# Copying the FFN's PSUM banks to SBUF on ScalarE before VectorE adds to them

## The chip, the cores and the metric

The kernel runs on one core of a Trainium2 chip. The time is the device time of one execution in microseconds (us), taken as the median over repeated executions. The profile is a single execution recorded by the hardware profiler; it has its own time, and a span from its first to its last instruction.

Five engines work in parallel, each on its own queue in order: TensorE (PE in the profile; its weight loads are PEld), VectorE (DVE), ScalarE (ACT), GpSimd (POOL) and SyncE (SP, which here only issues transfers). TensorE writes its products into PSUM, eight banks of 128 x 512 float32 values; VectorE and ScalarE read them from there. Everything else lies in SBUF. An engine that needs what another one made waits on a semaphore at the head of its queue, and all that stands behind it in that queue waits too.

## The reference, cut to what matters

Input `x` has 2048 tokens of 512 channels. Two branches are computed from it and mixed by a gate per token:

```
g = sigmoid((x * gate_w).sum(-1, keepdims=True))
q, k, v = split(x @ wqkv)                      # 32 heads of 16 channels
idx = pos[:, None] - arange(8)[None, :] * 2    # each token sees 8 tokens, 2 apart
logits = where(idx >= 0, einsum(q, k[idx]) * 16**-0.5, -1e9)
a = einsum(softmax(logits), v[idx]) @ wo
b = (gelu(x @ w_gate) * (x @ w_up)) @ w_down   # 512 -> 1792 -> 512
return g * a + (1 - g) * b
```

All data are float32.

## The kernel before, in words

**Tokens and passes.** The tokens are taken in two passes (`par` 0 and 1: the even and the odd ones), 1024 tokens each. A pass projects keys and queries (`project`, `qkv_mm`, L247), then values (`values`, L298), and then runs the FFN (`ffn`). The attention itself is done by VectorE (`scores`, `softmax`, `mix`, L390 to L453) and is written as one long generator, `attention`. `pull` takes pieces of it between the FFN's pieces, so that VectorE's attention work lies beside TensorE's FFN work over nearly the whole run.

**Float32 on TensorE.** Each operand is split into a high part and a remainder, and a product takes three matmuls (high x high, low x high, high x low).

**The FFN's first half.** `ffn` loops over 14 tiles `f` of 128 hidden columns; each calls `gate_up`. There the tokens (two halves of 512), the channels (two halves of 256) and the columns (gate and up) form a 2 x 2 by 2 x 2 block product, which is done with seven block products instead of eight. One block product, `product` (L600 to L606, its matmuls on L605), is six matmuls 128 x 128 by 128 x 512 into one bank. The operands of the tokens are `A` tiles (plain blocks a11, a12, a22) and `S` tiles (sums s1 to s4); the weights lie in `g0` and `g1`. The order in one tile `f` is:

1. `X_` = a11 b11; ScalarE copies it into a second bank `W_` (L680).
2. `Z_` = s1 t1; ScalarE copies it to SBUF as `p5` (`copy`, L610).
3. `fourth()`: the seventh product of the tile before, a22 t4, is added into that tile's `X_`; ScalarE applies gelu to it (L711), and `hidden` follows.
4. `X_` += s2 t2; ScalarE copies it to SBUF as `u2`.
5. `W_` += a12 b21; ScalarE applies gelu (L695), giving `c11`.
6. `Z_` += s4 b22; then `c12 = add(Z_, u2)`.
7. `X_` += s3 t3; then `c22 = add(X_, p5)`; `X_` stays in use until step 3 of the next tile.

`add` (L613 to L616) is called twice for each tile, 28 times in a pass and 56 times in all. It takes a tile of the pool `c` (four buffers) for its result. The bank that it reads can be written again only when the read is over: `Z_` goes back into the rotation of four banks called `p`, and the seventh product goes on adding into `X_`.

`hidden` (L618 to L623) multiplies the gelu by the up part on VectorE (L619), takes the high part on ScalarE (`hh`, L621) and the remainder on VectorE (`hl`, L622).

**The FFN's second half.** `down` (L634 to L660) multiplies `hh` and `hl` by the down weights `d` (matmuls on L645). For half the tokens the sums stay in the banks `acc0` to `acc3`; for the other half they go through `p` banks that ScalarE fills from SBUF (L639) and empties again into `rt` (L658). The pieces of `down` stand between the steps above.

**Other ScalarE work in a tile.** It makes the weights' parts for the tiles ahead: `operands` (L554, L562, L565) and `down_w` (L591, L595, L598). Keys and queries of the second half of the heads are copied out of their banks on L268 and sent to HBM on SP's queue (L271), from which `load_kq` (L379, L382) and `load_slots` bring them back for the attention. VectorE makes the other part of `g0` on L558 and sums of weights on L534.

**What sets the order.** The program is written in the order above, but the framework's scheduler places each engine's instructions by its own timeline when the kernel is built, so an edit can move instructions on any queue. `paced` ties an instruction to the last matmul written before it, for the scheduler alone.

Of the kernel before, what the change touches and what calls it, by code (L numbers as in the profile page):

```python
# [12 lines left out]
AF = mybir.ActivationFunctionType  # L13
OP = mybir.AluOpType
# [30 lines left out]
def tile_gated_mix(ctx: ExitStack, tc: tile.TileContext, xt, wqkv, wff, wo, out):  # L45
    nc = tc.nc
# [10 lines left out]
    def tl(tag, dt=F32):  # L57
        return pool.tile([P, COLS.get(tag, 512)], dt, name=tag, bufs=BUFS[tag])
# [5 lines left out]
    def bank(tag):  # L64
        return psum.tile([P, 512], F32, name=tag, bufs=BUFS.get(tag, 1))
# [545 lines left out]
        return s  # L611

    def add(ps, s):  # L613
        c = tl("c")[:, :512]
        nc.vector.tensor_tensor(c, ps, s, op=OP.add)  # L615
        return c  # L616

    def hidden(key, ge, up):  # L618
# [43 lines left out]
    def gate_up(par, f, pieces, do):  # L662
# [33 lines left out]
        idle(5, 0.7)  # L696
        product(Z_, "s4", w["b22"], False)
        c12 = add(Z_, u2)
        idle(6, 0.5)
        piece(2)  # L700
        product(X_, "s3", w["t3"], False)
        c22 = add(X_, p5)
        hidden((f, 0), c11, c12)
        idle(7, 0.7)
# [180 lines left out]
    def finish(oT):  # L885
        def add(u, jj):
            half, t = divmod(jj, BT)
            by_unit(ACC[jj], oT[u, half], u, t, False, u == NU - 1)

        for u in range(NU - 1):  # L890
            need_o(1, u + 1)
            for half in range(2):
                oT[u + 1, half] = channels(1, u + 1, half)
            if u + 2 < NU:
                for jj in range(NP):
                    add(u, jj)
                pull(4.0)

        for jj in range(BT):
            add(NU - 2, jj)  # L900
        for jj in range(NP):
            if jj >= BT:
                add(NU - 2, jj)
            add(NU - 1, jj)
            pa = ACC.pop(jj)
            r = tl(("s", "rt")[jj % 2])
            if jj % 2 and jj < NP - 1:
                nc.vector.tensor_copy(r, pa)
            else:
                nc.scalar.activation(r, pa, AF.Copy)  # L910

            cols = ((nc.scalar, 0, 256), (nc.sync, 256, 512)) if jj == NP - 1 else ((nc.sync, 0, 512),)
            for queue, a, b in cols:
                queue.dma_start(out_v[2 * jj + 1, :, a:b], r[:, a:b])
# [21 lines left out]
    ps = [bank(next(names)) for _ in range(NP)]  # L936
# [108 lines left out]
```

## Time and profile before

| | |
|---|---|
| median of 3 runs | 614.03 us (612.59 to 614.57) |
| profiled execution | 614.4 us, its span 612.6 us |
| TensorE busy, 2791 matmuls | 599.9 us, 98% of the span |
| VectorE busy, 624 instructions | 531.1 us, 87% |
| ScalarE busy, 643 instructions | 375.6 us, 61% |
| chain that ended last | PE 79%, DVE 7%, DMA 7%, ACT 3%, issue 3% |
| mean granted TensorE clock | 0.994 |

A row of a group reads: line, engine, operation, output<-inputs, sizes, count | busy us, mean ns of one | idle us of the engine just before them, and what ended it. A row of the timeline reads: start us, us, engine, line, operation, output<-inputs, count, and in brackets the idle time before it with its releaser. The ends of matmuls are modelled: consecutive ones overlap in the rows, so their pace is read from their starts. Instructions of VectorE and ScalarE overlap their neighbours in the rows by about 0.1 us as well.

### The profile page before, as it was taken

To read this page: it belongs to the slowest core of one execution; us is meant where nothing else is said; L and a number is where in the kernel's file an instruction comes from. 1 tells how busy PE (TensorE), PEld (TensorE's weight loads), DVE (VectorE), ACT (ScalarE), POOL (GpSimd) and SP (SyncE) were. 2 spreads that over 40 slices of the span, in tenths; PEclk is the share of its full clock that TensorE was granted. 3 is DMA by queue.
4 is the path that set the end of the run, shared out by engine and by line. 5 is a ranking of instruction groups with operands and counts; after the bars stand their busy time and mean duration, and the time that the engine had idled before them with its cause. 6 is when DMAs were issued, how large, how long until landed. Compare 5 with 4: busy or idle time off the path is not lost.

```text
span 612.6 us, 8147 instructions
## 1 busy us (share of the span) xinstructions
PE 599.9 (98%) x2791; PEld 499.8 (82%) x2791; DVE 531.1 (87%) x624; ACT 375.6 (61%) x643; POOL 69.0 (11%) x94
## 2 busy tenths in 40 slices
PE   8999988999999999999999999999999999999997
PEld 7898866888788887888899888888888887888885
DVE  6949889898999969985969998999896979998961
ACT  6665554576676686565486338466765686686632
POOL 0140000111010111101100002111011111101300
PEclk9999997999999999999999999999999999999999
DMA  8695995868688876896779949886698587937724
GB/s 288 241 268 172 296 288 178 234 188 252 175 236 217 241 217 173 254 278 193 276 210 317 285 160 287 223 236 163 222 213 253 121 255 169 289 87 205 95 61 156
DMA packets 85592, 132.80 MB, mean 217 GB/s; under 512 B 8111, under 2 KB 50223, under 8 KB 85550
## 3 DMA queue, kind: packets, MB, share of 16 engines
q1 hardware_dynamic: 66190, 100.88, 49.8%
q0 software_dynamic: 10368, 26.81, 22.9%
q10 hardware_dynamic: 8992, 4.59, 2.5%
q8 instruction: 22, 0.36, 0.2%
q14 instruction: 20, 0.16, 0.1%
HBM read 69.83 MB, written 40.46 MB: 180 GB/s over the span
## 4 chain that ended last, share of the span: by engine, by line
PE 79%; DVE 7%; DMA 7%; ACT 3%; issue 3%; SPq 0%; DVEq 0%; ACTq 0%
PE p L605 36%; PE acc L645 11%; PE p L645 11%; PE acc L247 7%; PE p L867 5%; PE p L247 3%; PE acc L298 2%; PE p L298 2%; PE acc L867 2%; DVE prod L398 2%; DMA ks<-hh 2%; DVE prod L436 1%; DMA v<-vs 1%; DMA kq<-kq 1%; DMA kq<-qs 1%
## 5 line engine op out<-in xcount | busy, mean ns | idle before, releaser
L605 PE MATMUL p<-S,g 128*128 128x512 f32 x672 | 168.4, 393 | 0.8 <-DVE c L615 0.8
L605 PEld LDWEIGHTS p<-S,g 128*128 128x128 f32 x672 | 127.3, 190 | 28.0 <-DVE c L615 1.5
L605 PE MATMUL p<-A,g 128*128 128x512 f32 x504 | 128.3, 392 | 3.4 <-DVE c L615 2.6
L605 PEld LDWEIGHTS p<-A,g 128*128 128x128 f32 x504 | 94.5, 189 | 24.8 <-DVE c L615 3.8
L398 DVE TENSOR_TENSOR prod<-kq 128x2048 f32<-128x2048 f32 x32 | 72.8, 2276 | 6.3 <-DMA kq<-kq 3.7
L436 DVE TENSOR_TENSOR prod<-v,lg 128x2048 f32<-128x2048 f32 x32 | 72.9, 2277 | 3.0 <-DMA v<-vs 2.2
L401 DVE TENSOR_REDUCE lg<-prod 128x128 f32<-128x2048 f32 x32 | 72.9, 2279 | 0.1
L645 PE MATMUL p<-d,hh 128*128 128x512 f32 x224 | 68.6, 389 | 0.0
L645 PE MATMUL acc<-d,hh 128*128 128x512 f32 x224 | 60.2, 390 | 2.1 <-ACT d L591 2.1
L563 POOL DMA_DIRECT2D g<-raw x28 | 24.2, 865 | 273.6 <-ACT g L562 157.5
L645 PEld LDWEIGHTS acc<-d,hh 128*128 128x128 f32 x224 | 42.0, 188 | 11.1 <-ACT d L591 2.5
L645 PEld LDWEIGHTS p<-d,hh 128*128 128x128 f32 x224 | 42.0, 188 | 8.7
L619 DVE TENSOR_TENSOR c<-c 128x512 f32<-128x512 f32 x56 | 38.2, 683 | 11.9 <-ACT c L711 11.8
L615 DVE TENSOR_TENSOR c<-p,s 128x512 f32<-128x512 f32 x56 | 37.6, 683 | 7.1 <-PE p L605 7.0
L621 ACT ACTIVATE hh<-c 128x512 fp32r<-128x512 f32 x56 | 35.1, 627 | 12.5 <-DVE c L619 12.4
L622 DVE TENSOR_TENSOR hl<-c,hh 128x512 fp32r<-128x512 f32 x56 | 38.3, 684 | 4.6 <-ACT hh L621 4.5
L610 ACT ACTIVATE s<-p 128x512 f32<-128x512 f32 x56 | 33.1, 596 | 14.7 <-PE p L605 14.5
L645 PE MATMUL p<-d,hl 128*128 128x512 f32 x112 | 42.1, 389 | 0.0
L658 ACT ACTIVATE rt<-p 128x512 f32<-128x512 f32 x48 | 27.9, 594 | 23.1 <-PE p L645 22.6
L565 ACT ACTIVATE g<-raw 128x1024 fp32r<-128x1024 f32 x28 | 29.7, 1060 | 19.8 <-PE p L605 19.6
L596 POOL DMA_DIRECT2D d<-r x26 | 22.4, 873 | 151.3 <-ACT d L595 97.2
L440 DVE TENSOR_TENSOR prod<-prod 128x1024 f32<-128x1024 f32 x32 | 39.0, 1219 | 0.2
(174 smaller groups left out, 938.2 us busy)
## 6 DMA issues: line engine op xcount, KB each, us to landing
g<-raw POOLq DMA_DIRECT2D x28, 512.0 KB, 6.1
raw<-wff SPq DMA_DIRECT2D x42, 256.0 KB, 3.6
ws<-g SPq DMA_DIRECT2D x14, 768.0 KB, 5.2
g<-ws SPq DMA_DIRECT2D x14, 768.0 KB, 6.1
r<-wff SPq DMA_DIRECT2D x28, 256.0 KB, 3.5
d<-r POOLq DMA_DIRECT2D x26, 256.0 KB, 6.1
v<-vs SPq DMA_DIRECT2D x8, 512.0 KB, 6.9
os<-tb SPq DMA_DIRECT2D x64, 64.0 KB, 3.3
```

What stands on the lines that cost most here:

```text
L247: LAST[:] = [nc.tensor.matmul(ps[:, :cn], a[:, t], w[:, c0:c0 + cn], start=(kc == 0 and n == 0), stop=(kc == KC - 1 and n == 2))]
L398: paced(nc.vector.tensor_tensor(prod, spans(k, jj), q[:, jj:jj + 2, None, :].to_broadcast([P, 2, W, UC]), op=OP.mult))
L401: nc.vector.tensor_reduce(two_of(lg, jj), prod.rearrange("p j w (h d) -> p (j w) h d", d=DH), axis=AX.X, op=OP.add)
L436: paced(nc.vector.tensor_tensor(prod.rearrange("p j w (h d) -> p (j w) h d", d=DH), spans(v, jj).rearrange("p j w (h d) -> p j w h d", d=D ...
L440: nc.vector.tensor_tensor(prod[:, :, :4], prod[:, :, :4], prod[:, :, 4:], op=OP.add)
L605: LAST[:] = [nc.tensor.matmul(ps, w_, a_, start=(start and kc == 0 and n == 0), stop=(kc == 1 and n == 2), skip_group_check=True)]
L615: nc.vector.tensor_tensor(c, ps, s, op=OP.add)
L619: nc.vector.tensor_tensor(ge, ge, up, op=OP.mult)
L621: nc.scalar.activation(hh_, ge, AF.Copy)
L622: nc.vector.tensor_tensor(hl_, ge, hh_.bitcast(F32), op=OP.subtract)
L645: LAST[:] = [nc.tensor.matmul(pp, a[:, ts], w, start=(i == 0 and n == 0 and gr == 0), stop=(i == 1 and n == 2), skip_group_check=True)]
L867: LAST[:] = [nc.tensor.matmul(pa, a, b, start=(first and n == 0), stop=(last and n == 2), skip_group_check=True)]
```

## The change

ScalarE copies the bank into the tile `c`, and VectorE adds the other summand to that tile in place. Everything else is written as before; line numbers behind `add` grow by two.

```diff
     def add(ps, s):
+
         c = tl("c")[:, :512]
-        nc.vector.tensor_tensor(c, ps, s, op=OP.add)
+        nc.scalar.activation(c, ps, AF.Copy)
+        nc.vector.tensor_tensor(c, c, s, op=OP.add)
         return c
```

In the program as built, ScalarE has 56 more copies (and one table load fewer, 17 instead of 18); VectorE, TensorE, GpSimd and SyncE have as many instructions as before. Of the 56 copies 25 stand in ScalarE's queue directly in front of L565 (those for `c12`) and 23 directly in front of L598 (those for `c22`). TensorE's seventh product, which waited for VectorE's add, waits for ScalarE's copy.

## The prediction

> **What bounds the kernel now.** I read the page's busy times first, then the costliest groups, then who waited for the changed line, and last the timeline at each place where TensorE stood still. Times are us.
>
> ```profile
> span 612.6 us, 8147 instructions
> PE 599.9 (98%) x2791; PEld 499.8 (82%) x2791; DVE 531.1 (87%) x624; ACT 375.6 (61%) x643; POOL 69.0 (11%) x94
> ...
> L605 PE MATMUL p<-S,g 128*128 128x512 f32 x672 | 168.4, 393 | 0.8 <-DVE c L615 0.8
> ...
> L605 PE MATMUL p<-A,g 128*128 128x512 f32 x504 | 128.3, 392 | 3.4 <-DVE c L615 2.6 <-DVE g L558 0.8
> ...
> L619 DVE TENSOR_TENSOR c<-c 128x512 f32<-128x512 f32 x56 | 38.2, 683 | 11.9 <-ACT c L711 11.8
> L615 DVE TENSOR_TENSOR c<-p,s 128x512 f32<-128x512 f32 x56 | 37.6, 683 | 7.1 <-PE p L605 7.0
> ...
> L610 ACT ACTIVATE s<-p 128x512 f32<-128x512 f32 x56 | 33.1, 596 | 14.7 <-PE p L605 14.5
> ```
>
> TensorE is the bound: busy 98% of the span. So nothing that the change does to VectorE or ScalarE counts by itself; what counts is where TensorE waits. The two L605 groups name the changed line as the releaser of nearly all of their idle time. The view of that line says the same:
>
> ```profile
> L615 DVE TENSOR_TENSOR c<-p,s x56: 672/682/692, 66.5 to 556.5; 128x512 f32<-128x512 f32 x56
> ...
>   PE p L605: 7.0, 10
> ...
>   PE p L605: 3.4, 4
> ```
>
> VectorE waited for the bank 10 times out of 56; TensorE waited for VectorE's add 4 times. The timeline has those four, each with the matmuls ahead of it, and the chain of waits has an undisturbed run for the pace:
>
> ```profile
> 128.18 6.80 PE p L605 x30
> ...
> 92.77 2.02 PE L605 MATMUL p<-A,g 128*128 128x512 f32 x4 [0.80 <-DVE g L558]
> 95.57 4.92 PE L605 MATMUL p<-S,g 128*128 128x512 f32 x12 [0.78 <-DVE c L615]
> ...
> 157.93 1.52 PE L605 MATMUL p<-A,g 128*128 128x512 f32 x6
> 160.28 1.65 PE L605 MATMUL p<-A,g 128*128 128x512 f32 x6 [0.83 <-DVE c L615]
> ...
> 233.85 1.52 PE L605 MATMUL p<-A,g 128*128 128x512 f32 x6
> 236.53 1.67 PE L605 MATMUL p<-A,g 128*128 128x512 f32 x6 [1.16 <-DVE c L615]
> ...
> 509.29 1.52 PE L605 MATMUL p<-A,g 128*128 128x512 f32 x6
> 511.39 1.66 PE L605 MATMUL p<-A,g 128*128 128x512 f32 x6 [0.59 <-DVE c L615]
> ```
>
> The pace is 6.80/30 = 0.227 for a matmul. The loss at a stall is the start after it, less the start before it, less six matmuls (1.36), plus the stretch of the first six after it over 1.52: at 160, 0.99 + 0.13 = 1.12; at 236, 1.32 + 0.15 = 1.47; at 511, 0.74 + 0.14 = 0.88. Together 3.47. The fourth is in a stretch of half clock, below.
>
> **Why VectorE is late there.** The product was done, but VectorE was in the middle of a 2.3 us attention multiply:
>
> ```profile
> 232.99 2.29 DVE L436 TENSOR_TENSOR prod<-v,lg 128x2048 f32<-128x2048 f32 x1
> 235.20 1.28 DVE L615 TENSOR_TENSOR c<-p,s 128x512 f32<-128x512 f32 x2
> ```
>
> The two adds run back to back, so both banks had been waiting. ScalarE's long instructions take about 1 us (L565, part 2), and at 61% busy it is mostly waiting for TensorE when a bank is done.
>
> **Part 1: the add on VectorE.** It keeps its 683 ns: L619, which adds nothing but SBUF tiles of this size, also takes 683, so reading SBUF in place of PSUM saves nothing. Taken at 0. Bounds: -56 x 0.011 to +56 x 0.009 by the spread 672 to 692, some 0.6 either way, all on VectorE and under TensorE's cover.
>
> The Trainium skill speaks against the edit: "VectorE: DVE Perf Modes", section "Rules for kernel authors", says for elementwise work on a matmul's output to accept the slow read from PSUM, or to copy first where many operations follow; here one follows. The rows agree that the add gets no cheaper. By that rule alone nothing is won and the costs below remain, 614.03 + 0.8 = 614.8; I go by the waits, since what the copy buys is the bank's earlier release.
>
> **Part 2: the copy on ScalarE.** The same operation and shape is L610, 596 ns. Back to back it adds less:
>
> ```profile
> L565 ACT ACTIVATE g<-raw 128x1024 fp32r<-128x1024 f32 x28 | 29.7, 1060 | 19.8 <-PE p L605 19.6
> ...
> 114.39 1.09 ACT L658 ACTIVATE rt<-p 128x512 f32<-128x512 f32 x2 [1.63 <-PE p L645]
> ...
> 171.26 1.06 ACT L565 ACTIVATE g<-raw 128x1024 fp32r<-128x1024 f32 x1 [1.71 <-PE p L605]
> 172.23 0.58 ACT L658 ACTIVATE rt<-p 128x512 f32<-128x512 f32 x1
> ...
> 174.27 0.60 ACT L658 ACTIVATE rt<-p 128x512 f32<-128x512 f32 x1 [0.79 <-PE p L645]
> ...
> 174.01 2.88 PE L605 MATMUL p<-A,g 128*128 128x512 f32 x12
> ```
>
> Two take 1.09, so one more adds 0.49; 56 x 0.49 = 27 us, ScalarE's share going to about 66%. In the new queue order the copies stand directly in front of L565 (25 of them) and L598 (23). At L565 ScalarE has waited for that very product, 19.6 over 28 instructions, 0.70 each, and 1.71 in the tile shown; so the copy finds ScalarE free and is done 0.6 after the product. What it pushes: L565 and the first L658 by 0.49, from an end at 172.81 to 173.30; the matmuls that take the bank it frees start at 174.01, so 1.20 of margin becomes 0.71. The second L658 has idle time of 0.79 before it and absorbs the rest. Cover: that margin. Without it a tile would lose up to 0.49, and 1.20 at most if both copies and L565 fell together. I take 0, since the copies stand where ScalarE had to wait for the same products, and what they push still ends before it is wanted; 0.5 for a tile is rival C's price.
>
> **Part 3: the stalls go.** The seventh product now waits for ScalarE. From the end of the product of `c22` to it TensorE has some 12 matmuls of other work (2.7 us), and the copy needs 0.6. So the three stalls at full clock go: -3.47. Bounds: 0 (all come back elsewhere, rival B) to -3.47.
>
> **Part 4: the stall at 95.** Three rows by clock (stretch in us, length, busy us and count of PE, PEld, DVE, ACT, POOL, granted clock, DMA share, GB/s) and the row of the wait ahead:
>
> ```profile
> 90.77 1.20 PE L645 MATMUL acc<-d,hh 128*128 128x512 f32 x4 [2.06 <-ACT d L591]
> ...
> 89.00:92.80 3.80, 1.23 (x5) 0.70 (x5) 3.80 (x5) 3.58 (x6) 0.00 (x0) 1.00 0.35 91
> 92.90:96.30 3.40, 2.62 (x6) 1.61 (x7) 3.40 (x4) 0.58 (x1) 0.00 (x0) 0.50 0.65 234
> 96.30:99.60 3.30, 3.30 (x10) 2.54 (x9) 3.30 (x4) 0.60 (x1) 0.00 (x0) 0.50 0.87 315
> ```
>
> TensorE stands still for 2.06 and 0.80 at 88 to 92.8, and then runs at half clock until 99.6. Neither wait is on L615 (they are on L591 and L558), so both stay. The wait on L615 goes: four matmuls from 92.77 at half pace, about 4.92/12 = 0.41 each, end at 94.41, and the next started at 95.57: -1.15. Bounds: 0 to -1.2.
>
> **Part 5: what the first copy pushes.** The first copy of all is in front of the copies of the keys to SBUF (L268), for which SP's queue waits. In the chain:
>
> ```profile
> 64.17 0.95 ACT g L565
> ...
> 65.63 9.61 DMA ks<-hh
> ...
> 75.26 5.92 DMA kq<-qs
> ```
>
> ScalarE runs without a pause there, so this store starts 0.49 later, and with it the load of the next keys and queries, the attention multiply behind it, and the stall at 90.77. +0.49; bounds 0 (the transfers lie too dense for the store's start to matter) to +0.6.
>
> **Part 6: VectorE starts some adds later.** Where VectorE waited for the bank (10 times) it now waits for the copy too, +0.63 each, 6 us on an engine with 81 us idle. Behind the add stand the multiply L619, the high part L621 and `hl`. The tightest consumer that I found next to a removed stall:
>
> ```profile
> 159.66 0.63 ACT L621 ACTIVATE hh<-c 128x512 fp32r<-128x512 f32 x1 [2.25 <-DVE c L619]
> ...
> 161.77 1.52 PE L645 MATMUL acc<-d,hh 128*128 128x512 f32 x6
> ```
>
> `hh` ends at 160.29 and is wanted at 161.77: margin 1.48, of which 1.12 goes when TensorE comes that much earlier. 0.36 is left, against a delay of 0 (VectorE already late) to 0.63. I charge 0.3 for all such places; bounds 0 to 4 x 0.6 = 2.4.
>
> **Sum,** against the profiled execution's own 614.4: -3.47 - 1.15 + 0.49 + 0.3 = -3.8, so 610.6. The median of 614.03 is 0.4 below the profiled execution, so the median after should be 610.2.
>
> **Rivals.**
> - *B, the wait only moves.* TensorE no longer waits for the bank, but VectorE is as late as before, and TensorE waits for `hh` or `hl` instead. For: VectorE is 87% busy and in order, and the margin left at 160 is 0.36. Against: at 511 `hh` ends at 513.73 and is wanted at 516.97 (rows below), 3.24 for a stall of 0.88. Then nothing of 4.6 is kept and parts 5 and 6 are paid: 614.03 + 0.8 = 614.8.
>
> ```profile
> 513.10 0.63 ACT L621 ACTIVATE hh<-c 128x512 fp32r<-128x512 f32 x1 [1.68 <-DVE c L619]
> ...
> 516.97 1.52 PE L645 MATMUL acc<-d,hh 128*128 128x512 f32 x6
> ```
>
> - *C, slower: ScalarE's queue releases the `p` banks late.* The pair of copies pushes L658 by up to 2 x 0.49 = 0.98 where its idle time is gone, and TensorE waits for the bank. It decides where the margin is under 0.98; at 174 it is 1.20, and at 114 the two L658 end at 115.48 with their bank wanted at 115.77 (row below), 0.29. If half of the 24 tiles with these releases were as tight, 12 x (0.98 - 0.29) = 8.3: 614.03 - 4.6 + 0.8 + 8.3 = 618.5. Against: before that pair ScalarE sat idle for 1.63.
>
> ```profile
> 115.77 1.52 PE L605 MATMUL p<-S,g 128*128 128x512 f32 x6
> ```
>
> - *D, the half clock ends sooner.* Clock 0.50 held over two stretches of 3.4; in the first TensorE was busy 2.62 of 3.40, in the second wholly, and then the clock was full. Without the wait on L615 the first could be busy nearly throughout and full clock return after it: 3.4/0.41 = 8 matmuls, each 0.41 - 0.227 = 0.18 shorter, -1.5: 608.7. Against: the waits ahead stay and move by 0.49 into it. The Trainium skill, "TensorE: Matmul & The Clock Gate", section "What's actually happening", has this rule: full clock after one busy window of about 3.4 us, and the windows run freely of the kernel. The trace agrees that a wholly busy 3.30 came right before the release; no run here yet shows whether 77% is too little.
>
> **Chances.** The forecast 0.50, D 0.15, B 0.20, C 0.15. A measurement of this kernel tells about 0.3% (1.84) from no change: below 612.2 is faster, above 615.9 slower. So faster 0.65, same 0.20, slower 0.15. The range goes from 608.0, a little under D, to 614.8, B's time, which leaves out C and a little under D.
>
> **What would show it.** No PE wait on the add's line or on the copy's at 160, 236 and 511, and L605's idle time down from 4.2 to about 1. VectorE's 683 ns unchanged. ScalarE busy about 33 us more, with L565 and L598 idle before them turned into idle before the copy. The wait on L591 near 90 a little longer. Wrong would be: PE idle before L645 on `hh` or `hl` (B), PE idle on L658's successor (C), another length of the half clock (D).

## The result, and the profile after

The changed kernel takes 606.21 us (median of 4 runs, 604.73 to 606.99) against 613.31 for the kernel before beside it: ratio 0.989, 95% interval 0.9845 to 0.9935. The forecast was 610.2 in a range of 608.0 to 614.8, so the sign was right and the gain, 7.1 for a forecast of 3.8, was about twice as large. The profiled execution took 606.67 us.

The page's first lines and its costliest groups answer to those of before; `add` is now L616 (the copy) and L617 (the add), and lines behind it have moved by two:

```profile
span 604.9 us, 8190 instructions
PE 596.3 (99%) x2791; PEld 498.9 (82%) x2791; DVE 530.8 (88%) x624; ACT 400.6 (66%) x698; POOL 68.6 (11%) x94
...
L605 PE MATMUL p<-S,g 128*128 128x512 f32 x672 | 167.6, 389 | 0.0
...
L605 PE MATMUL p<-A,g 128*128 128x512 f32 x504 | 126.6, 389 | 0.8 <-DVE g L558 0.8
...
L616 ACT ACTIVATE c<-p 128x512 f32<-128x512 f32 x56 | 33.4, 597 | 32.8 <-PE p L605 32.7
...
L617 DVE TENSOR_TENSOR c<-c,s 128x512 f32<-128x512 f32 x56 | 38.3, 686 | 6.4 <-ACT c L616 6.1
```

L605's idle time fell from 4.2 to 0.8, and none of it is on the add or on the copy. Of the copies VectorE waited for 7 (6.1 us); TensorE's matmuls waited for none. The view of the groups by line shows where ScalarE's 33 us came from, the kernel before first and the changed one second:

```profile
L565 ACT ACTIVATE g<-raw 128x1024 fp32r<-128x1024 f32 x28 | 29.7, 1060 | 19.8 <-PE p L605 19.6
L658 ACT ACTIVATE rt<-p 128x512 f32<-128x512 f32 x48 | 27.9, 594 | 23.1 <-PE p L645 22.6
L598 ACT ACTIVATE d<-r 128x512 fp32r<-128x512 f32 x26 | 16.3, 630 | 9.3 <-PE p L605 9.2
```

```profile
L565 ACT ACTIVATE g<-raw 128x1024 fp32r<-128x1024 f32 x28 | 29.5, 1053 | 0.0
L598 ACT ACTIVATE d<-r 128x512 fp32r<-128x512 f32 x26 | 16.2, 628 | 0.0
L660 ACT ACTIVATE rt<-p 128x512 f32<-128x512 f32 x48 | 28.2, 594 | 8.4 <-PE p L647 8.1
```

The idle time in front of L565 and L598 is gone; it now stands in front of the copy. The idle time in front of the release of the `p` banks (L658, now L660) fell as well, from 23.1 to 8.4.

Next, who kept TensorE waiting (total us, times, longest), before and then after:

```profile
PE p L605 <- DVE c L615: 3.4, 4, 1.2
PE acc L645 <- ACT d L591: 2.1, 1, 2.1
...
```

```profile
PE acc L647 <- ACT d L591: 1.3, 1, 1.3
PE p L247 <- ACT rt L86: 1.3, 1, 1.3
PE p L72 <- DVE warm L69: 1.0, 1, 1.0
PE p L605 <- DVE g L558: 0.8, 1, 0.8
```

The four waits on the add are gone and no new one stands in their place. But they are not all of the difference: TensorE's clock never fell to half inside this execution, as it had for 6.8 us in the one before. In every profiled execution of this study the clock kept a state, from one change to the next, for a multiple of 3.41 us (the 6.83 here are two of them). I call such a stretch a window, and count windows back from where the clock changed. The rows of the view by stretches are those of the prediction (stretch, length, busy us and count of PE, PEld, DVE, ACT, POOL, granted clock, DMA share, GB/s), cut at the windows; before:

```profile
89.45:92.86 3.41, 1.29 (x5) 0.76 (x5) 3.41 (x4) 3.22 (x6) 0.00 (x0) 1.00 0.30 85
92.86:96.27 3.41, 2.63 (x6) 1.62 (x7) 3.41 (x4) 0.58 (x1) 0.00 (x0) 0.50 0.63 229
```

After:

```profile
88.18:91.59 3.41, 2.08 (x10) 1.42 (x9) 3.41 (x4) 2.33 (x5) 0.00 (x0) 1.00 0.61 129
91.59:95.01 3.42, 2.61 (x12) 1.75 (x11) 3.42 (x4) 2.81 (x5) 0.00 (x0) 1.00 0.29 80
```

Before, one window held TensorE's waits on L591 and L558 together and TensorE was busy for 1.29 of it; half clock followed. After, the same two waits lie on either side of a window's edge, and nothing followed.

The sum nearly closes with that. In the half-clock stretch 14 matmuls ran (the counts 6 and 10 of the prediction's rows hold two of them twice, since these lie across the edge between the rows). By their starts, from 96.17 to 99.16 for seven, their pace was 0.427, so each took 0.427 - 0.227 = 0.20 longer: 2.8. With the stalls of parts 3 and 4, 3.47 + 1.15 + 2.8 = 7.4. The profiled executions differ by 614.4 - 606.67 = 7.7.

### The profile page after: what moved, and what is told of

Same layout as the page of the kernel before. It is cut to its first block, busy times and chain, and to the rows that moved or that the text cites. A ratio compares the mean times of both kernels' runs of the same rounds, so it can differ in the third digit from the quotient of the medians.

```text
span 604.9 us, 8190 instructions
## 1 busy us (share of the span) xinstructions
PE 596.3 (99%) x2791; PEld 498.9 (82%) x2791; DVE 530.8 (88%) x624; ACT 400.6 (66%) x698; POOL 68.6 (11%) x94
## 4 chain that ended last, share of the span: by engine, by line
PE 90%; DMA 6%; DVE 2%; SPq 1%; issue 1%; ACT 0%; ACTq 0%; DVEq 0%
PE p L605 42%; PE p L647 13%; PE acc L647 12%; PE acc L247 8%; PE p L869 5%; PE p L247 3%; PE acc L298 3%; PE p L298 2%; PE acc L869 2%; DMA kq<-kq 1%; DVE prod L398 1%; DMA kq<-qs 1%; DMA raw<-xt 1%; DMA ks<-hh 1%; DMA vs<-hh 1%; DMA vs<-hl 1%
## 5 line engine op out<-in xcount | busy, mean ns | idle before, releaser
L605 PE MATMUL p<-S,g 128*128 128x512 f32 x672 | 167.6, 389 | 0.0
L605 PEld LDWEIGHTS p<-S,g 128*128 128x128 f32 x672 | 125.9, 188 | 26.3 <-ACT p L682 0.3
L605 PE MATMUL p<-A,g 128*128 128x512 f32 x504 | 126.6, 389 | 0.8 <-DVE g L558 0.8
L605 PEld LDWEIGHTS p<-A,g 128*128 128x128 f32 x504 | 94.3, 188 | 20.8 <-DVE g L558 1.2
L401 DVE TENSOR_REDUCE lg<-prod 128x128 f32<-128x2048 f32 x32 | 73.0, 2281 | 0.1
L616 ACT ACTIVATE c<-p 128x512 f32<-128x512 f32 x56 | 33.4, 597 | 32.8 <-PE p L605 32.7
L617 DVE TENSOR_TENSOR c<-c,s 128x512 f32<-128x512 f32 x56 | 38.3, 686 | 6.4 <-ACT c L616 6.1
L647 PE MATMUL acc<-d,hl 128*128 128x512 f32 x112 | 37.1, 389 | 0.0
```

What stands on the lines that cost most here:

```text
L401: nc.vector.tensor_reduce(two_of(lg, jj), prod.rearrange("p j w (h d) -> p (j w) h d", d=DH), axis=AX.X, op=OP.add)
L605: LAST[:] = [nc.tensor.matmul(ps, w_, a_, start=(start and kc == 0 and n == 0), stop=(kc == 1 and n == 2), skip_group_check=True)]
L617: nc.vector.tensor_tensor(c, c, s, op=OP.add)
L647: LAST[:] = [nc.tensor.matmul(pp, a[:, ts], w, start=(i == 0 and n == 0 and gr == 0), stop=(i == 1 and n == 2), skip_group_check=True)]
```

## The experiments

The expectations name theories by letters. P: the half clock comes where TensorE's standstill near 90 us meets the clock's windows, so in some executions only; L: it comes in each. S: the gain is the new order of the queues, not the bank's release. C is the prediction's rival C. The other letters are explained where they stand. Each kernel was timed beside the kernel before on the same chip. Clocks are means over an execution. One window at half clock takes 0.0028 from the mean (half of 3.41 in some 610 us). Half clock at the end of the span, after the last matmul, took at most 0.0019 in the 14 profiled executions (2.37 us). So 0.998 and above means no window at half clock while matmuls ran, and 0.996 and below at least one. The counts below are of the clearer ends, 0.999 and above and 0.995 and below.

**How steady the kernel before is.** No edit.

> The kernel before, unchanged, as its own comparison: how often does TensorE fall to half clock near 93 us, and what does that cost? Theory P (the half clock depends on where the clock's windows lie in the execution, beside the length of the standstill at 88): some executions with a mean granted clock of about 0.994 and some with 0.999 or 1.0, the latter about 3 us shorter (16 matmuls at 0.41 instead of 0.227); the ratio to the kernel before is 1.000. Theory L (the standstill of 2.06 and 0.80 us always brings it on): every execution at about 0.994, and all within 2 us of each other.

It took 612.08 (609.13 to 614.42, 12 runs), ratio 0.9989 (0.9969 to 1.001). Its profiled execution took 609.76 and had no half clock:

```profile
88.07:91.48 3.41, 2.14 (x9) 1.15 (x8) 3.41 (x4) 2.92 (x5) 0.00 (x0) 1.00 0.32 88
91.48:94.89 3.41, 1.82 (x8) 1.19 (x7) 3.41 (x4) 0.58 (x1) 0.00 (x0) 1.00 0.82 275
```

Here TensorE waited 0.5 on L591 where it had waited 2.06, and 3.3 on the add, in three places in place of four:

```profile
93.89 3.02 PE L605 MATMUL p<-S,g 128*128 128x512 f32 x12 [1.59 <-DVE c L615]
...
231.96 1.66 PE L605 MATMUL p<-A,g 128*128 128x512 f32 x6 [1.16 <-DVE c L615]
```

The third, of 0.58, is near 507; the stall near 160 did not occur. So the half clock, the wait on L591 and the stall at 160 are no fixed parts of this kernel. Over the 107 executions of the kernel before that are compared in this study, the median was 612.08; 43 had a clock of 0.999 or above (median 610.58), and 25 had 0.995 or below (median 613.31). Only 6 of the 107 took longer than the 614.03 that the prediction started from.

**Half of the edit: only `c22`, and only `c12`.**

```diff
-    def add(ps, s):
+    def add(ps, s, by_act):
         c = tl("c")[:, :512]
-        nc.vector.tensor_tensor(c, ps, s, op=OP.add)
+        if by_act:
+            nc.scalar.activation(c, ps, AF.Copy)
+            nc.vector.tensor_tensor(c, c, s, op=OP.add)
+        else:
+            nc.vector.tensor_tensor(c, ps, s, op=OP.add)
...
-        c12 = add(Z_, u2)
+        c12 = add(Z_, u2, False)       # the other kernel: True
...
-        c22 = add(X_, p5)
+        c22 = add(X_, p5, True)        # the other kernel: False
```

> ScalarE copies only the bank of c22 (X_, which the seventh product waits for); c12 is added from the bank by VectorE as before. Theory (ScalarE frees the bank sooner than VectorE): the waits at 160, 236 and 511 go, 3.5 us; a wait on the add of c12 near 95 can stay. 28 copies more on ScalarE. About 609.5, or some 3 less where the half clock doesn't come. Rival S (the gain is in the schedule that ScalarE's and SP's queues got, not in the release): the three waits stay, time as before.

> ScalarE copies only the bank of c12 (Z_); c22 is added from the bank by VectorE. Theory: the three waits at 160, 236 and 511, all of them of the seventh product into X_, stay, so between 612 and 614; only the wait near 95 goes (1.15). Rival S: as fast as the whole change, 606 to 607, if half of the copies move the queues in the same way.

The copy for `c22` alone: 608.07, ratio 0.9934 (0.9912 to 0.9957), with a wait of 0.2 on the add left in all. The copy for `c12` alone: 611.37, ratio 0.9976 (0.9953 to 0.9998). In its timeline one of the three stalls that were expected to stay is left, the one near 230, still on the add:

```profile
230.61 1.65 PE L605 MATMUL p<-A,g 128*128 128x512 f32 x6 [1.17 <-DVE c L619]
```

The stall near 160 is missing in an execution of the unchanged kernel too; why the one near 507 went with `c12` alone isn't shown. The half clock of this execution did not come near 93: it followed a wait of 2.24 on a transfer (`g<-raw`) at 372.

By the times the greater part comes from `c22`, whose bank the seventh product goes on adding into, as the prediction had it. The copy for `c12` adds 1 to 2 us to it (608.07 against 606.1, with intervals that overlap).

**The same work on ScalarE, but the bank released by VectorE.** ScalarE copies the bank onto itself, and VectorE adds from the bank as before.

```diff
         c = tl("c")[:, :512]
+        nc.scalar.activation(ps, ps, AF.Copy)
         nc.vector.tensor_tensor(c, ps, s, op=OP.add)
```

> ScalarE copies the bank onto itself (its value stays as it is) and VectorE then adds from the bank: the same 56 ScalarE instructions at the same place in the chain, but the bank is still released by VectorE's add. Theory: the waits of TensorE on the add stay or grow, since the add can start only 0.6 us later: 614 to 618. Rival S: 606 to 608, since ScalarE's queue is the same as in the changed kernel.

615.11, ratio 1.0046 (1.0023 to 1.0068): slower than before. The groups and TensorE's waits:

```profile
L615 ACT ACTIVATE p<-p 128x512 f32<-128x512 f32 x56 | 32.8, 586 | 18.2 <-PE p L605 18.2
...
L616 DVE TENSOR_TENSOR c<-p,s 128x512 f32<-128x512 f32 x56 | 37.9, 683 | 5.4 <-ACT p L615 5.3
```

```profile
PE p L605 <- DVE c L616: 3.4, 4, 1.6
PE p L247 <- ACT rt L86: 1.6, 1, 1.6
PE p L605 <- ACT rt L659: 1.2, 2, 0.7
...
```

The copies cost ScalarE what they cost in the changed kernel, and TensorE still waited 3.4 for VectorE's add. S falls as far as this kernel can tell: with the same copies, but without the earlier release, the waits stay and there is no gain. It is not a clean test of the release alone, since the add, and with it the release, also comes later by the copy, and the scheduler plans each kernel anew, so that TensorE's order is not the changed kernel's.

**The copy twice.**

```diff
-        nc.scalar.activation(c, ps, AF.Copy)
+        for _ in range(2):
+            nc.scalar.activation(c, ps, AF.Copy)
```

> The changed kernel with every copy issued twice, the second over the first: twice what the change costs ScalarE, with VectorE's add and the release of the bank behind both. My theory (the copies fall in ScalarE's idle time, the tightest consumers having 0.7 us of margin): ScalarE's busy time up by 27 to 33 us to about 430, and the time 606 to 608.5, since a second 0.49 fits into most margins. Rival C (ScalarE's queue releases the p banks late, hidden so far by a small margin): waits of TensorE on ScalarE's lines in many tiles, 0.3 to 0.5 in each of 12 or more, time above 610.

614.91, ratio 1.0063 (1.0029 to 1.0096), which is 8.8 above the changed kernel. My expectation of 606 to 608.5 was wrong. ScalarE was busy 425.4, 24.8 more. TensorE's waits:

```profile
PE p L605 <- DMA g<-raw: 2.1, 1, 2.1
PE p L247 <- ACT rt L86: 1.7, 1, 1.7
PE p L605 <- ACT rt L660: 1.5, 1, 1.5
PE acc L647 <- ACT d L591: 1.1, 1, 1.1
PE p L72 <- DVE warm L69: 1.0, 1, 1.0
PE p L605 <- ACT c L616: 0.9, 1, 0.9
...
```

A `p` bank (L660), a copy and a transfer (`g<-raw`) came late, and the wait on that transfer was followed by a window of half clock from 372.80 to 376.21. All of TensorE's waits in this view come to 9.3, against 4.4 in the changed kernel's, and the end of the span after the last matmul was 1.8 longer (613.14 - 607.30 = 5.84 for 4.07). Only the wait on L660 is rival C's mechanism, and it came once, in one tile, not in the 12 that C counted on. The wait on the transfer is not shown to come from the second copy, since the kernel with the copy for `c12` alone has it too. Still, ScalarE's cover held one copy for each add, and not two.

**The changed kernel again.** No edit; it shows how often the half clock occurs.

> The changed kernel unchanged, with more executions: how often does TensorE's clock fall to half, and what is the ratio then? So far none of 4 executions showed a mean granted clock under 0.999, while about two thirds of the executions of the kernel before did. Theory P (the half clock needs a long standstill near 90 us, whose length varies with the landing of a load and whose position varies against the clock's own windows): the changed kernel still stands still there for 1.33 us, so some executions, between 0 and 4 of 10, come at a clock of 0.993 to 0.997 and take 2.5 to 3 us longer than the rest; median 606 to 607.5, ratio 0.988 to 0.992. Rival F (the removed wait at 95 is what made the half clock, so it is gone for good): no execution under 0.999, 605 to 606.5.

606.11 (605.15 to 607.43, 6 runs), ratio 0.992 (0.9892 to 0.9948). Of all 10 executions 8 had 0.999 or above, one 0.998 and one 0.996 (607.2): theory P. F, that it is gone for good, does not hold, though by one execution only.

**L591 earlier, in both kernels.** The conversions that TensorE waits for at 90 are issued ahead of the `hh` that they stood behind. VectorE's order is the same as without the move.

```diff
-                    at(2 if f > 2 else 4, next, steps, None)
+                    at(2 if f > 2 or f == 1 and not par else 4, next, steps, None)
```

> The changed kernel with the two conversions of L591 (the weights `d` of the first two pieces) issued ahead of the `hh` that waits for the attention multiply, instead of behind it. The order of VectorE stays as it was. Theory P: the wait on L591 near 90 (1.33 in the changed kernel's trace) goes, the wait on L558 stays at about 0.8 to 1.5 since VectorE is as late as before, the half clock appears in no execution; 604.8 to 606.0, some 1 us less than the changed kernel and with no executions at a low clock. Rival W (the wait only moves: TensorE arrives earlier at the wait on L558 and waits there longer by the same amount): L558's wait at 1.9 to 2.2, time as the changed kernel's.

> The kernel before with only that move of L591, and VectorE's adds reading the bank as before. It tells the two parts of the gain apart. Theory P: the half clock goes or becomes rare (clock 0.999 to 1.0 in at least 8 of 10 executions against about 4 of 10 before), the three waits on the add at 160, 236 and 511 stay with about 3.3 of idle time; 609 to 610.5, which is the time of the kernel before at full clock less up to 1. Rival F (the half clock comes from the wait on the add at 95): low clocks as often as before, median 611.5 to 613.

In the changed kernel: 606.87, ratio 0.9925 (0.9899 to 0.9951), with 4 of 7 executions at 0.999 or above. In the kernel before: 613.37, ratio 1.0026 (1.0004 to 1.0048), with none of 12. Both expectations of P failed, and W, that the wait only moves, is right. In the kernel before, the low clocks that F expected came, and more often than it expected. In the timelines, the changed kernel and then the kernel before:

```profile
92.45 3.95 PE L605 MATMUL p<-A,g 128*128 128x512 f32 x10 [2.01 <-DVE g L558]
```

```profile
92.46 1.19 PE L605 MATMUL p<-A,g 128*128 128x512 f32 x4 [2.02 <-DVE g L558]
95.26 5.49 PE L605 MATMUL p<-S,g 128*128 128x512 f32 x12 [1.61 <-DVE c L615]
```

Two waits with matmuls between them had become one, of 2.0, and in the kernel before half clock became more frequent (none of 12 at 0.999 or above, against 43 of 107); for the changed kernel 4 of 7 against 8 of 10 tell nothing. In the kernel before, the wait on the add follows after only four matmuls:

```profile
90.67:94.08 3.41, 1.19 (x4) 0.67 (x4) 3.41 (x4) 0.98 (x2) 0.00 (x0) 1.00 0.39 108
94.08:97.49 3.41, 2.23 (x5) 1.82 (x6) 3.41 (x6) 0.25 (x1) 0.00 (x0) 0.50 0.95 354
97.49:100.91 3.42, 3.42 (x9) 2.64 (x8) 3.42 (x5) 0.72 (x2) 0.00 (x0) 0.50 0.47 153
```

So it isn't the sum of the waits that counts, but how much of one window they take. A window with so little TensorE work is called starved below.

**L558 earlier too.** With L591 early as above, the step of L558 is moved as well: in the changed kernel ahead of the reduction L401, in the kernel before only ahead of `hl`.

```diff
-                    at(5 + i, next, steps, None)
+                    at(3 if f == 1 and not (par or i) else 5 + i, next, steps, None)   # before: 4
```

> The changed kernel with L591 ahead of the `hh` that waits for the attention multiply, and L558 (the low part of the weights of the third piece) ahead of the reduction L401 on VectorE instead of behind it and behind `hl`. By the times of the changed kernel's trace L558 then ends near 90.2 instead of 92.9, about when the conversion's four matmuls are done. Theory P (the standstill between 88 and 93 sets the half clock, the rest is its own length): both waits together fall from 2.1 to under 0.6, no execution has the half clock, 604.0 to 605.3. Rival W (the wait moves on to `hl`, which now comes later, or to the attention's next load): a wait of 1 to 2 appears between 90 and 100 on another line and the time stays at 606.

> The kernel before with the early L591 and with L558 in front of `hl` on VectorE (0.68 earlier), the adds reading the bank as before. Against the run with the early L591 alone, which had one wait of 2.0 on L558 and a mean clock of 0.994 to 0.997 in all 12 executions, this one has a wait of about 1.3 there. Theory P with a threshold (a window of the clock that is mostly idle brings the half clock): the half clock becomes rarer, some executions at 0.999 to 1.0, median 610.5 to 612. Rival R (where the order of L591 is changed the half clock comes whatever the length of the wait): clocks stay at 0.994 to 0.997 and the time at 612.7 to 613.5.

The changed kernel with it: 605.68, ratio 0.9902 (0.9868 to 0.9935), no half clock in 6 executions. W held again: the waits on L591 and L558 are gone and one of 1.7 on a copy has come, in front of which ScalarE waited 0.56 for the store of an earlier `c` tile. It is the lowest median, but not to be told from the changed kernel's. The kernel before with it: 612.09, ratio 1.0004 (0.9983 to 1.0025), with 1 of 12 executions at 0.999 or above. P failed here too. Its rival R, that the early L591 brings the half clock whatever the length of the wait, fits these clocks but not the time (612.7 to 613.5 expected), and the trace shows another reason. The wait on L558 was 1.3, as expected, but TensorE then came earlier to the wait on the add, and that one starved the window:

```profile
91.40 1.19 PE L605 MATMUL p<-A,g 128*128 128x512 f32 x4 [1.29 <-DVE g L558]
94.80 4.61 PE L605 MATMUL p<-S,g 128*128 128x512 f32 x12 [2.21 <-DVE c L615]
```

**The wait at 95 alone.** This points to the wait on the add near 95, which the change removes, as one of the half clock's causes. So two kernels differ from these in just that place: the changed kernel with the two adds of that piece (of 56) reading the bank again, and the kernel before with a copy for these two only. `add` takes `by_act` as above.

```diff
-        c12 = add(Z_, u2)
+        c12 = add(Z_, u2, par or f != 1)          # the reverse: not par and f == 1
...
-        c22 = add(X_, p5)
+        c22 = add(X_, p5, par or f != 1)          # the reverse: not par and f == 1
```

> The changed kernel in which only the two adds of the piece worked on between 85 and 95 us read the bank again; the other 54 are as changed. Read from the runs so far: a window of TensorE's clock (3.41 us) in which it was busy for at most 1.78 was followed by half clock, one with at least 1.82 by full clock; at 88 to 95 three waits (L591, L558, and the add's) fell into two windows before the change, and two waits after it. Theory T (the add's wait near 95 is the one of the three that makes a starved window likely): the wait on the add comes back with 0.8 to 2.2, the mean clock is 0.994 to 0.997 in more than half of the executions, against 1 of 10 for the changed kernel; time 607.5 to 610. The order of later work shifts a little, so the clock tells more than the time. Rival U (the changed kernel's half clock is rare for another reason, the position of the waits in the windows or work elsewhere): clocks as the changed kernel's, at least 8 of 10 at 0.999 to 1.0, time 606 to 607.5.

> The reverse: the kernel before in which only these two adds have their copy; the other 54 read the bank. Theory T: the wait on the add near 95 goes, at least 8 of 10 executions at a clock of 0.999 to 1.0, the three stalls at 160, 236 and 511 stay with about 3.3 of idle time; time 609 to 610.5, which is the time of the kernel before at full clock less about 1. Rival U: the mean clock at 0.994 to 0.998 in about two thirds of the executions, as before, 611 to 612.5.

The changed kernel without these two: 610.05 (607.81 to 612.51), ratio 0.9982 (0.9963 to 1.0001), 5 of 12 executions at 0.999 or above and 3 at 0.995 or below. The kernel before with only these two: 609.20 (607.27 to 612.75), ratio 0.9955 (0.9934 to 0.9976), 8 of 12 at 0.999 or above and none at 0.995 or below. By the times T, that this wait makes the starved window likely, holds in the second and misses its range by 0.05 in the first; U, that the half clock is rare for another reason, holds in neither. By the clocks the counts lean to T but do not show it: the kernel before beside them on that chip had 13 of 23 at 0.999 or above, and against that neither 5 of 12 nor 8 of 12 is clear of chance. The windows and the waits of the first:

```profile
90.11:93.53 3.42, 1.30 (x5) 0.67 (x4) 3.42 (x3) 1.39 (x2) 0.00 (x0) 1.00 0.41 119
93.53:96.94 3.41, 3.12 (x7) 2.51 (x8) 3.41 (x6) 0.15 (x1) 0.00 (x0) 0.50 0.95 336
```

```profile
PE p L605 <- DVE c L617: 1.6, 1, 1.6
...
PE acc L647 <- ACT d L591: 0.9, 1, 0.9
```

And a window of the second kernel, in whose profiled execution half clock came without the add's wait, from 1.66 on L591 and 0.80 on L558:

```profile
88.67:92.08 3.41, 1.19 (x4) 0.67 (x4) 3.41 (x3) 3.41 (x7) 0.00 (x0) 1.00 0.37 97
```

Two adds of 56 were thus worth 2.5 us from the one side (611.67 beside it against 609.20), and 3.9 from the other (610.05 against 606.1, on another chip). Most of the 2.5 is the stall and not the half clock: at 0.999 and above alone the medians are 610.68 and 608.69, 2.0 apart. Up to the changed place each kernel has the order of the one it was made from, and behind it another: some of the 3.9 is that, since two waits on ScalarE of 0.7 and 0.8 are new.

## Why the prediction was right and wrong, point by point

- **What bounds it, part 3 and the mechanism: right.** TensorE waited on the add because VectorE was in a long multiply; ScalarE's copy releases the bank in time, and the stalls went. Copying onto the bank itself, with VectorE still the releaser, gained nothing. That there were three at full clock was the profiled execution's number; the next one of the same kernel lacked the stall at 160 and waited 1.59 near 95.
- **Part 1: right.** The add took 686 ns for 683. By the rule of the Trainium skill ("VectorE: DVE Perf Modes", section "Rules for kernel authors") copying first pays where many operations follow. Here one follows, VectorE saved nothing, and it paid all the same, through the release.
- **Part 2: right, with less cover than thought.** ScalarE took 25.0 us more (400.6 - 375.6), 0.45 a copy for the 0.49 forecast (with one table load of 1.28 fewer), and the idle time moved to where the prediction said. But a second 0.44 a copy cost 8.8 us. A margin read at one tile (0.71) didn't tell that.
- **Part 4: the step that failed.** The prediction said that the waits on L591 and L558 "both stay", and took the half clock from 92.9 to 99.6 as staying with them. The two waits did stay (1.33 and 0.81). The half clock mostly did not. It is no property of the two waits but of how they fall into the clock's windows, so it comes in some executions and not in others: of the kernel before, 43 of 107 were at 0.999 or above, of the changed kernel 8 of 10. Taking one profiled execution as the kernel hid this; that execution had two windows at half clock, worth 2.8. Why the half clock became rarer is shown only in part. In four kernels that keep the wait on the add near 95 it lay, wholly or in part, in a starved window (1.19, 1.20, 1.30 and 1.62 us busy), so removing it takes away one way into half clock; the counts of the two kernels made to test that wait alone are not clear of chance.
- **Part 5: not seen.** Forecast +0.49, from a store of the keys that ScalarE's copy delays. In the changed kernel's chain that store waits for SP's queue instead, and the load and the multiply follow it:

```profile
67.59 1.50 SPq L383
...
69.19 5.71 DMA ks<-hh
...
74.92 6.42 DMA kq<-qs
...
81.47 2.29 DVE prod L398
```

  And its timeline has TensorE behind it:

```profile
88.09 1.52 PE L605 MATMUL p<-S,g 128*128 128x512 f32 x6
90.95 1.19 PE L647 MATMUL acc<-d,hh 128*128 128x512 f32 x4 [1.33 <-ACT d L591]
```

  The multiply started at 81.47 for 81.30, but in other executions at 79.62 (the kernel before) and 79.90 (the changed one). So its start varies by 1.6 or more in the same kernel, and a single pair can't show a delay of 0.49 or its absence. The wait in front of TensorE got shorter, not longer as forecast, since TensorE came there 0.9 later (its last product ahead of the wait starts at 88.09 instead of 87.19).
- **Part 6: too dear.** +0.3 was charged for `hh` and `hl`; TensorE waited for neither in the profiled execution.
- **The sum.** At full clock alone the medians are 610.58 before (43 executions) and 606.11 after (8): -4.47. The forecast had -4.62 for the stalls and +0.79 for parts 5 and 6. So the stalls were right in sum, within a few tenths, and of the 0.79 little can have come; that the single stalls change from one execution to the next makes so close a fit partly luck. The miss of 4.0 is made of three parts, to about 0.1: the three executions behind 614.03 lay 1.95 above the median of the 107; the half clock in part of the executions, 612.08 - 610.58 = 1.5, was kept in the forecast and mostly went; and about 0.6 was charged too much. The low end of the range failed for the same reasons: it allowed one window at half clock to go, and not all.
- **The rivals.** B didn't happen in this kernel: there is no wait on `hh` or `hl`. A wait that only moves was seen where L591 and L558 were made earlier. C didn't happen, and with one more copy it came in one tile. D was the nearest, and was too small: it let the half clock end one window sooner (-1.5), where in most executions all of it went. Its question whether 77% busy is too little to end the half clock was answered by the prediction's own rows: a window with 2.62 of 3.40 busy was followed by another at half clock. The rule that the windows run freely of the kernel ("TensorE: Matmul & The Clock Gate", section "What's actually happening", in the Trainium skill) agrees with every profiled execution here: their edges lie at other times in each. The prediction used it to end the half clock, and not to ask how often it begins.

## What to carry to other kernels

A bank that a busy engine reads late can be worth a copy by an engine that is free just then, even if the copy saves the reader nothing; look at who releases it, and at how much of the copier's idle time is left for the next such step. Before a stretch of half clock is entered in a sum as staying or going, look at several executions: if their mean clocks differ, the price is a chance times a cost. A short wait can cost more than its length if it falls into the same 3.41 us window as other waits.

## What the runs showed of the hardware

Clock windows with TensorE much less than busy, over the profiled executions of all kernels here, while matmuls were left to do (the record of the clock begins 4 to 7 us into an execution, so the windows before that don't count): with 1.19, 1.19, 1.20, 1.29, 1.30, 1.30, 1.39, 1.62, 1.72 and 1.78 us busy of 3.41 half clock followed; with 1.82, 1.92, 1.93, 2.05, 2.06, 2.08 and more the clock stayed full. The two nearest to the edge are a start-up window of the kernel that copies in place, and the one of the unchanged kernel shown above:

```profile
4.67:8.08 3.41, 1.78 (x6) 0.74 (x5) 1.19 (x3) 0.60 (x1) 0.00 (x0) 1.00 0.97 325
```

So a window about half idle was enough; none was wholly idle. At half clock, windows with 2.23 and 2.63 busy were followed by another at half clock, and windows with 3.02 and more by full clock, among them this one of the changed kernel with L591 early:

```profile
92.06:95.47 3.41, 3.02 (x7) 2.44 (x8) 3.41 (x4) 0.81 (x2) 0.00 (x0) 0.50 0.51 157
```

The section of the Trainium skill named above ("TensorE: Matmul & The Clock Gate") says that full clock ends after an idle window of about 3.4 us and returns after a busy one. The runs agree in the length, and show how little idleness counts as idle. The first two edges, 1.78 and 1.82, were read off the earlier executions and written down before the last two kernels ran, which kept to them; the other two were read off afterwards. No run placed a window between 1.78 and 1.82, or between 2.63 and 3.02. What sets the varying landing of the load near 81, and with it the wait on L591 of 0.5 to 2.1, stays open.
